# A fourth PSUM pair kept in the ring through the second key projection, and another split of the wk copies between ScalarE and VectorE

## The chip, the cores and the metric

The kernel runs on one core of one Trainium2 chip. The metric is the device time of one execution in microseconds. The kernel before took 290.92 us (median of 3 runs, 290.85 to 291.63).

## The reference, cut to what matters

The program mixes a linear-attention block with a SwiGLU block, for 2048 tokens of width 640.

```python
    def _A_ref(x, wqkv, w_phi, wo):
        ...
        pk = jnp.einsum("bhsd,hdf->bhsf", k, w_phi)
        ...
        phi_k = jnp.concatenate([_softmax(pk, axis=-1), _softmax(-pk, axis=-1)], axis=-1)
        kv = jnp.einsum("bhsf,bhsd->bhfd", phi_k, v)
        ...
    def _B_ref(x, w_gate, w_up, w_down):
        g = _silu(x @ w_gate)
        u = x @ w_up
        return (g * u) @ w_down
    ...
    return g * a + (1 - g) * b
```

Both `k` and `w_phi` are linear, so the kernel multiplies the two weights once, in five chunks of 128 rows ("wk products", steps M0 to M4), and then projects the tokens with the product (steps K0 to K15).

## The kernel before: the parts that matter

The order in which work is issued is a list of steps. F is an FFN item (gate and up products, 512 tokens), M a wk product, V a value product, K a key projection, E a kv sum, Q a query projection, O the attention output, D the down projection, H warm-up matmuls. "I" takes one PSUM pair out of the ring. The loads are issued in their own order (f0, f1, f2 are column ranges of the FFN weights).

```python
LOADS = """
x0 w0 x1 w1 x2 w2 x3 w3 w4 f0 h k0 k1 t4 k2 k3 k4 t5 ... t15 q0 q1 q2 q3
q4 f1 f2
"""
ORDER = """
...
X3 U2.2 U0.3 U1.3 U2.3 U0.4 U1.4 U2.4 V3 Y F0.1 M1 i3 M0 I F0.0 M2 V4 M3 M4 K0 K1 S0 V6 V5 S1 P0
...
"""
```

The eight banks of PSUM are four pairs. A step takes the pair that was used longest ago; the kv sums own pair 3 from E0, the first of them, to the last; step I takes it out of the ring ahead of that.

```python
    ring = {"n": 4, "lru": [0, 1, 2, 3]}
    ...
    def next_pair():
        return used([r for r in ring["lru"] if r < ring["n"] and r not in held][0])
    ...
    def kv_begin():          # step I
        ring["n"] = 3
```

A wk product is six small matmuls and one copy out of PSUM. K0 reads the five products in turn, c = 0 to 4, two matmuls for each, and waits for each copy by itself.

```python
    def premult(which, m):
        pr = next_pair()
        ...
        mm(pairs)
        copy("dve" if which and m % 2 == 0 else "act", wqk[:, which, m, :].rearrange("p (b c) -> p b c", b=2), halves(pr))

    def tok_proj(t, which, split=False):
        pr = next_pair()
        pairs = [(bank(2 * pr + hb, 0, 320), xT[:, t, c, :], wqk[:, which, c, 320 * hb:320 * hb + 320],
                  c == 0, c == 4, False) for c in range(5) for hb in range(2)]
        if split:                                   # K0 only
            for c in range(5):
                mm(pairs[2 * c:2 * c + 2])
        ...
```

The softmax here doesn't subtract the row's maximum and nothing guards it: scores larger than these inputs give would overflow.

## Time and profile before

| | before |
|---|---|
| device time | 290.92 us |
| span of the profiled execution | 288.81 us |
| first matmul of F0.1 | 12.09 us |
| wk products M3, M4 start | 18.73, 19.43 us |
| K0, first kv sum start | 19.75, 27.95 us |
| waits of TensorE after 8 us, by the waits view | one, 0.2 us |

The device time contains about 1.8 us that the span does not; so the span is the part to explain.

From the page of before: span, engine row (busy us, share of the span, instructions), and the chain of work that ended last, by engine.

```profile
span 288.8 us, 4885 instructions
...
PE 285.2 (99%) x1977; PEld 174.7 (60%) x1977; DVE 162.8 (56%) x241; ACT 147.5 (51%) x251; POOL 160.5 (56%) x125
...
PE 96%; DMA 2%; DVE 1%; SPq 0%; ACT 0%; issue 0%
```

In the views PE is TensorE, PEld its weight loads, PEq its sequencer, DVE is VectorE, ACT ScalarE, POOL GpSimd, and SP SyncE, which issues the loads. TensorE sets the time. Its 99% must be read with care. The Trainium skill (Perfetto Trace Analysis, "Tensor Engine Instruction (MATMUL, LD_WEIGHTS)") says that the end of a matmul in the profile is an estimate. So I measure from start to start. The skill (TensorE: Matmul & The Clock Gate, "Wait — 56ns, not 53.3ns?") gives columns / 2.4 GHz + about 2.5 ns for a running array; this trace agrees: 20 matmuls of 320 columns take 2.72 us (0.136 each), 5 of 512 columns take 1.08 us (0.216 each). What a start is later than that is a hole.

The waits view of before, TensorE only:

```profile
engine line waited for: us in total, times, longest us
PE ps L471 <- PEq L773: 0.8, 1, 0.8
PE ps L294 <- DMA wvg<-in_A_wqkv_dram: 0.4, 2, 0.2
PE ps L294 <- DVE wqk L318: 0.2, 1, 0.2
PE ps L294 <- DVE xT L318: 0.2, 1, 0.2
```

The third line is the place that the change aims at. Around it, in the timeline of before (start us, duration us, engine, line, operation, out<-in, count, idle time before it and what ended that):

```profile
17.04 0.48 PE L294 MATMUL ps<-wbd,wT 128*128 128x140 bf16 x6
...
17.35 1.54 PE L294 MATMUL ps<-wvg,xT 128*128 128x320 bf16 x10
17.73 0.59 ACT L312 ACTIVATE us<-ps 128x512 bf16<-128x512 f32 x1
17.86 0.69 DVE L326 SCALAR_TENSOR_TENSOR hT<-hT,ps 128x512 bf16<-128x512 bf16 x1 [1.36 <-ACT hT L312]
18.47 0.81 DVE L318 CAST wqk<-ps 128x640 bf16<-128x640 f32 x1
...
18.73 0.48 PE L294 MATMUL ps<-wbd,wT 128*128 128x140 bf16 x6
18.93 0.71 ACT L312 ACTIVATE v1r<-ps 128x640 bf16<-128x640 f32 x1 [0.60 <-PE ps L294]
19.40 0.32 PEld L294 LDWEIGHTS ps<-wbd,wT 128*128 128x128 bf16 x6 [0.38 <-issue]
19.43 0.47 PE L294 MATMUL ps<-wbd,wT 128*128 128x140 bf16 x6 [0.23 <-DVE wqk L318]
19.53 0.17 ACT L312 ACTIVATE svec<-ps 128x1 f32<-128x1 f32 x1
19.58 0.71 ACT L312 ACTIVATE wqk<-ps 128x640 bf16<-128x640 f32 x1
...
19.75 1.40 PE L294 MATMUL ps<-wqk,xT 128*128 128x320 bf16 x9
19.94 0.82 DVE L318 CAST wqk<-ps 128x640 bf16<-128x640 f32 x1 [0.66 <-PE ps L294]
```

The first line is M2, then V4, M3 (18.73) and M4 (19.43). M1 and M0, one after the other, start about 0.31 us apart, so M4 could have started at 19.04. It starts 0.15 us after VectorE's copy of M2 (18.47 to 19.28): with three pairs M4 must write where M2 was. The profile's own "0.23" is smaller than the hole, because it counts from M3's modelled end; from start to start the hole is 0.39 us.

### The profile page before, as it was taken

What the parts mean: (1) busy time and instruction counts of PE and PEld (TensorE: products, weight loads), DVE (VectorE), ACT (ScalarE), POOL (GpSimd) and SP (SyncE); (2) the same over time, 40 slices, a digit from 0 to 9 for tenths busy, and PEclk for the clock granted to TensorE, in tenths of its full rate; (3) what the DMA queues carried; (4) which work ended last, traced back from release to release, by engine and by line L of the source; (5) the groups of instructions that cost most, each with busy time, mean ns of one, the idle gap of its engine ahead of it and who ended that gap; (6) DMA issues with size and microseconds to landing.
All of it is one profiled execution on the core that took longest, in us unless ns stands there. A gap on an engine that the chain in (4) does not pass through costs nothing.

```text
span 288.8 us, 4885 instructions
## 1 busy us (share of the span) xinstructions
PE 285.2 (99%) x1977; PEld 174.7 (60%) x1977; DVE 162.8 (56%) x241; ACT 147.5 (51%) x251; POOL 160.5 (56%) x125
## 2 busy tenths in 40 slices
PE   8999999999999999999999999999999999999997
PEld 6667777675644445557775546675454446656776
DVE  1256757486468987769992385980316799200000
ACT  1368768676674556574354663224675452234112
POOL 8276899879544798844733348450663649601000
DMA  6966789000010497302373102061020004410101
GB/s 214 174 119 129 108 229 353 5 2 1 0 49 0 75 330 137 70 10 41 62 141 85 20 0 51 2 134 57 2 50 0 2 1 82 92 45 0 48 23 48
DMA packets 48942, 21.61 MB, mean 75 GB/s; under 512 B 39384, under 2 KB 48792, under 8 KB 48920
## 3 DMA queue, kind: packets, MB, share of 16 engines
q1 hardware_dynamic: 48190, 20.62, 31.3%
q10 hardware_dynamic: 730, 0.68, 0.7%
q8 instruction: 16, 0.26, 0.4%
q14 instruction: 6, 0.05, 0.1%
HBM read 9.29 MB, written 2.62 MB: 41 GB/s over the span
## 4 chain that ended last, share of the span: by engine, by line
PE 96%; DMA 2%; DVE 1%; SPq 0%; ACT 0%; issue 0%
PE ps L294 96%; DMA wvg<-in_A_wqkv_dram 2%; SPq L348 0%; DVE wqk L318 0%; DVE hT L326 0%; ACT hT L312 0%; PE ps L306 0%; DVE osb L718 0%
## 5 line engine op out<-in xcount | busy, mean ns | idle before, releaser
L322 POOL TENSOR_TENSOR hT<-hT,us 128x512 bf16<-128x512 bf16 (+1 forms) x56 | 65.6, 1182 | 66.8 <-DVE hT L326 66.6
L326 DVE SCALAR_TENSOR_TENSOR hT<-hT,ps 128x512 bf16<-128x512 bf16 (+1 forms) x56 | 37.5, 683 | 73.5 <-ACT hT L312 61.2
L294 PE MATMUL ps<-xT,wg 128*128 128x512 bf16 x260 | 64.6, 379 | 0.0
L294 PE MATMUL ps<-xT,wu 128*128 128x512 bf16 x260 | 64.6, 379 | 0.0
L294 PE MATMUL ps<-wd,hT 128*128 128x320 bf16 (+2 forms) x462 | 63.9, 295 | 0.0
L312 ACT ACTIVATE hT<-ps 128x512 bf16<-128x512 f32 (+2 forms) x60 | 35.8, 596 | 46.5 <-PE ps L294 46.4
L322 POOL TENSOR_TENSOR ph<-eq,qc 128x1320 bf16<-128x1320 bf16 x16 | 42.4, 2648 | 26.1 <-DVE qc L631 24.0
L294 PEld LDWEIGHTS ps<-wd,hT 128*128 128x128 bf16 x462 | 44.5, 98 | 17.5 <-issue 0.2
L294 PE MATMUL ps<-wqk,xT 128*128 128x320 bf16 x320 | 47.7, 299 | 0.1
L294 PEld LDWEIGHTS ps<-xT,wu 128*128 128x128 bf16 x260 | 25.4, 98 | 30.7
L294 PEld LDWEIGHTS ps<-xT,wg 128*128 128x128 bf16 x260 | 25.0, 98 | 27.8 <-ACT oT L312 0.8
L312 ACT ACTIVATE osb<-ps,omg 128x640 bf16<-128x640 f32 (+2 forms) x17 | 12.9, 758 | 53.7 <-PE ps L294 53.7
L322 POOL TENSOR_TENSOR ekr<-ekr,krec 128x1280 bf16<-128x1280 bf16 x16 | 37.4, 2358 | 5.1 <-DVE krec L336 5.1
L294 PEld LDWEIGHTS ps<-wqk,xT 128*128 128x128 bf16 x320 | 30.5, 98 | 13.3 <-ACT us L312 0.5
L312 ACT ACTIVATE us<-ps 128x512 bf16<-128x512 f32 (+1 forms) x56 | 33.2, 593 | 0.3 <-POOL hT L322 0.2
L312 ACT ACTIVATE eq<-ps 128x640 bf16<-128x640 f32 x32 | 22.4, 704 | 17.3 <-POOL ph L322 10.4
L333 DVE TENSOR_REDUCE ksum<-ekr 128x64 f32<-128x1280 bf16 x16 | 23.5, 1470 | 10.4 <-ACT ekr L312 10.4
L312 ACT ACTIVATE ekr<-ps 128x640 bf16<-128x640 f32 x32 | 22.3, 704 | 8.6 <-PE ps L294 8.1
L294 PE MATMUL ps<-wvg,xT 128*128 128x320 bf16 (+1 forms) x160 | 24.6, 301 | 0.6 <-DMA wvg<-in_A_wqkv_dram 0.4
L333 DVE TENSOR_REDUCE qz<-eq 128x64 f32<-128x1280 bf16 x16 | 23.7, 1478 | 2.2 <-ACT eq L312 2.2
L294 PE MATMUL ps<-wog,oT 128*128 128x320 bf16 (+2 forms) x165 | 24.7, 294 | 0.0
L333 DVE TENSOR_REDUCE qw<-ez 128x64 f32<-128x1280 bf16 x16 | 23.6, 1477 | 0.0
(73 smaller groups left out, 188.6 us busy)
## 6 DMA issues: line engine op xcount, KB each, us to landing
out_dram<-osb SPq DMA_DIRECT2D x15, 160.0 KB, 1.9
wd<-in_B_w_down_dram SPq DMA_DIRECT2D x1, 2080.0 KB, 10.4
wg<-in_B_w_gate_dram SPq DMA_DIRECT2D x1, 1040.0 KB, 9.5
wu<-in_B_w_up_dram SPq DMA_DIRECT2D x1, 1040.0 KB, 10.5
wg<-in_B_w_gate_dram SPq DMA_DIRECT2D x1, 800.0 KB, 5.6
wu<-in_B_w_up_dram SPq DMA_DIRECT2D x1, 800.0 KB, 7.2
wog<-in_A_wo_dram SPq DMA_DIRECT2D x2, 375.0 KB, 7.1
wvg<-in_A_wqkv_dram SPq DMA_DIRECT2D x4, 160.0 KB, 4.5
```

Source lines behind the costliest of these rows:

```text
L294: last = pe.matmul(o, lhsT=l, rhs=r, start=st, stop=sp_, skip_group_check=sk)
L312: return run("act", lambda: act.activation(o, i, func, scale=scale), rd, [o])
L322: return run(e, lambda: eo.tensor_tensor(o, a, b, op), [a, b], [o])
L326: return run("dve", lambda: dve.scalar_tensor_tensor(out=o, in0=a, scalar=s, in1=b, op0=op0, op1=op1), rd, [o])
L333: return run("dve", lambda: dve.tensor_reduce(o, i, AX.X, ALU.add), [i], [o])
```

## The change

Its intent: let the fourth pair work until K1 has taken its own, so that M4 does not wait for M2's copy; and give the copies of M2 and M4 to ScalarE, M3's to VectorE, so that the copies come in the order in which they are wanted. No instruction is added; on balance one copy moves from VectorE to ScalarE.

```diff
-X3 U2.2 U0.3 U1.3 U2.3 U0.4 U1.4 U2.4 V3 Y F0.1 M1 i3 M0 I F0.0 M2 V4 M3 M4 K0 K1 S0 V6 V5 S1 P0
+X3 U2.2 U0.3 U1.3 U2.3 U0.4 U1.4 U2.4 V3 Y F0.1 M1 i3 M0 F0.0 M2 V4 M3 M4 K0 K1 I S0 V6 V5 S1 P0
...
-        copy("dve" if which and m % 2 == 0 else "act", wqk[:, which, m, :].rearrange("p (b c) -> p b c", b=2), halves(pr))
+        copy("dve" if which and m in (0, 3) else "act", wqk[:, which, m, :].rearrange("p (b c) -> p b c", b=2), halves(pr))
```

## The prediction

> **What bounds the kernel.** TensorE. The page's busy table gives PE 285.2 of 288.8 us (99%); the chain of waits is 96% matmuls. The Trainium skill (Perfetto Trace Analysis, Identifying the Most-Contended Engine) warns that matmul busy time says little about headroom, because matmuls are pipelined. So I took the distances between matmul starts in the timeline: 512-column matmuls follow each other at about 0.215 us, 320-column ones at about 0.135 us, nearly everywhere. After the first loads (about 8 us) I find one real hole, 0.39 us before the last wk product M4 (start 19.43 us, "DVE wqk"), one of 0.24 us at 128.9 us, and some below 0.1 us.
>
> **What makes the hole.** With the ring cut to three pairs before F0.0, M4 must write into M2's pair. Timeline: M2 runs at 17.04 us; its copy belongs to VectorE, which is first busy with F0.0's gate product (17.86 to 18.55) and copies M2 from 18.47 to 19.28. M3 is issued by about 19.04; M4 starts at 19.43, some 0.15 us after the copy's end.
>
> **What the change does.** The matmuls and their order stay the same; one wk copy moves from VectorE (0.82 us) to ScalarE (0.71 us).
> 1. Fourth pair until K1. Following the least-recently-used ring by hand, M4 then takes F0.0's pair, whose last reader ends at 18.55, and K0 takes M2's. M4 can start straight after M3, at about 19.04 (its weights landed at about 18.5), and K0 at about 19.35 instead of 19.75.
> 2. New split (VectorE: M0, M3; ScalarE: M1, M2, M4). K0 reads the wk products as its chunks 0 to 4. ScalarE copies M2 at about 18.2 to 18.9, in idle time before V4's copy, then M4 at about 19.58 to 20.29. VectorE is free for M3 at about 19.25 to 20.07. Chunk 3 is due at 19.35 + 6 x 0.135 = 20.16, chunk 4 at about 20.43; adding 0.15 us from a copy's end to the matmul, they are there at about 20.2 and 20.44. So K0 may stall 0 to 0.1 us. The split mainly frees M2's pair (now K0's) by about 19.0 instead of 19.28, which would be just before K0 needs it.
>
> **On the critical path:** estimate 0.39 - 0.04 = about 0.35 us. After K1 the assignment of pairs is the old one with names exchanged, so no wait is new. Later loads land at least 0.5 us before use: V6's token block at 21.3 us against 22.1, the last FFN weights at 51.4 against about 53. So PE's later work should move forward by 0.35 us, to the end.
>
> **Predicted time:** 290.92 - 0.35 = 290.57 us, say 290.6; range 290.1 to 291.0 (runs of before differ by 0.8 us among themselves, so the gain is of the size of the noise). Faster by over 2%: 0.5%; within 2%: 98.5%; slower by over 2%: 1%.
>
> **Right, if:** M4 follows M3 without the hole, and "PE <- DVE wqk" goes from PE's waits, or shrinks below 0.1 us inside K0; K0 starts at about 19.35 us; later PE landmarks (first kv sum, 27.95 us; Q7, 128.9 us) come 0.3 to 0.4 us earlier; span about 288.45 us. Wrong, if the hole reappears inside K0 (waiting for the copies of M3 or M4), or the lead is lost at a later load or at 128.9 us.
>
> **What would make it wrong:** loads arriving later in the first 20 us, which shift everything by some tenths; copies slower than 0.71 and 0.82 us when ScalarE and VectorE read PSUM together, making K0 wait; drift between sessions larger than the gain.

## The result, and the profile after

| | before | changed |
|---|---|---|
| device time, 6 runs each, median | 290.86 us | 290.91 us |
| lowest, highest | 290.07, 291.63 | 290.13, 291.47 |
| span of the profiled execution | 288.81 us | 288.36 us |
| F0.1's first matmul to the end of the span | 276.72 us | 276.32 us |

The ratio is 1.0004, with a 95% interval of 0.9981 to 1.0027. The timing shows no difference; a gain of 0.40 us would be a ratio of 0.9986, which lies inside the interval. The trace, on the other hand, shows the forecast gain.

The waits view of the changed kernel, TensorE only:

```profile
engine line waited for: us in total, times, longest us
PE ps L471 <- PEq L773: 0.8, 1, 0.8
```

The timeline of the changed kernel, same columns:

```profile
16.99 0.48 PE L294 MATMUL ps<-wbd,wT 128*128 128x140 bf16 x6
...
17.82 0.69 DVE L326 SCALAR_TENSOR_TENSOR hT<-hT,ps 128x512 bf16<-128x512 bf16 x1 [1.37 <-ACT hT L312]
18.16 0.71 ACT L312 ACTIVATE wqk<-ps 128x640 bf16<-128x640 f32 x1
...
18.68 0.79 PE L294 MATMUL ps<-wbd,wT 128*128 128x140 bf16 x12
18.88 0.71 ACT L312 ACTIVATE v1r<-ps 128x640 bf16<-128x640 f32 x1
19.20 0.82 DVE L318 CAST wqk<-ps 128x640 bf16<-128x640 f32 x1 [0.69 <-PE ps L294]
...
19.31 1.79 PE L294 MATMUL ps<-wqk,xT 128*128 128x320 bf16 x12
19.48 0.17 ACT L312 ACTIVATE svec<-ps 128x1 f32<-128x1 f32 x1
19.53 0.71 ACT L312 ACTIVATE wqk<-ps 128x640 bf16<-128x640 f32 x1
```

M3 and M4 are now one unbroken group of twelve matmuls (18.68), K0 starts at 19.31, and its matmuls follow each other without a break. M2's copy is ScalarE's (18.16), M3's is VectorE's (19.20), M4's is ScalarE's (19.53). The two traces differ by 0.05 us when F0.1 starts (12.09 and 12.04) and by 0.45 us at the first kv sum (27.95 and 27.50), at Q7 (128.91 and 128.46) and at the end.

So the question is the reverse of the usual one: the mechanism is plain in the trace, and the time does not show it. Where is it lost? Three theories stood at this point.

- **A:** the 0.40 us are saved in every execution, and the spread between executions (1.6 us) hides them. The spread comes from the first 12 us.
- **B:** the hole or its removal depends on the execution; in ordinary ones nothing is saved.
- **C:** TensorE is earlier, but waits for something later in some executions.

### The profile page after: what moved, and what is told of

It is laid out like the page before. It is cut to its first block, busy times and chain, and to the rows that moved or that the text cites. A ratio compares the mean times of both kernels' runs of the same rounds, so it can differ in the third digit from the quotient of the medians.

```text
span 288.4 us, 4884 instructions
## 1 busy us (share of the span) xinstructions
PE 285.5 (99%) x1977; PEld 175.2 (61%) x1977; DVE 162.1 (56%) x240; ACT 148.1 (51%) x252; POOL 160.5 (56%) x125
## 4 chain that ended last, share of the span: by engine, by line
PE 99%; DVE 0%; issue 0%
PE ps L294 97%; PE ps L471 1%; PE ps L306 1%; DVE osb L718 0%
```

## The experiments

In each I measured two things: the timed runs, and in the trace the distance from F0.1's first matmul to the end of the span, which leaves out the start.

### 1. More warm-up matmuls: does the spread come from the first loads?

88 warm-up matmuls ahead of the first transposes, the same edit in both kernels, so that the loads are there before TensorE asks.

```diff
-    def warm():
+    def warm(count=NWARM):
...
-            for _ in range(NWARM):
+            for _ in range(count):
...
-        "H": lambda i: warm(), ...
+        "H": lambda i: warm(90 if i == 12 else NWARM), ...
```

For the kernel before:

> The kernel before, with 88 more warm-up matmuls ahead of the first transposes, so that the first loads have landed before TensorE needs them. Theory A (the hole of 0.39 us is there in every execution and its removal reaches the end; the spread of up to 1.6 us between executions comes from the arrival of the first loads): 5 to 9 us slower than before, spread of its runs far below that of before (under 0.4 us), TensorE waits between 4 and 9 us of the old time scale gone, the 0.39 us hole before M4 still there. Rival B (spread is not from the loads, but from later, or from the launch): spread stays about 1 us. Rival C (the hole itself depends on when the loads come): the hole changes or is gone.

For the changed kernel:

> The changed kernel with the same 88 warm-up matmuls. Theory A: against q_before in the same rounds 0.3 to 0.5 us shorter, now outside the spread of both; no hole before M4 or K0. Rival B or C (the gain of the profile is lost again in ordinary executions): q_after and q_before agree within 0.1 us.

Measured: before with the edit 295.97 us median (295.23 to 296.33, 4 runs), changed with the edit 295.8 us (294.75 to 296.26, 5 runs). From F0.1 to the end: 276.72 and 276.32 us, to 0.01 us what they were. The hole before M4 is there in one (0.39 us) and gone in the other.

So the hole belongs to the kernel and not to the moment at which loads arrive: B lost ground. But the spread did not shrink (1.1 and 1.5 us), so my source for it was wrong, and the timed difference (0.28 us between the means) lies within it. The traces show what I had missed. In both, the warm-up matmuls start 0.107 us apart at first and 0.059 us apart later; the last slow one is at 5.49 us in one and at 6.77 us in the other, and the first value product follows at 10.54 and 11.11 us. The moment at which TensorE doubles its rate differs from execution to execution. The Trainium skill (TensorE: Matmul & The Clock Gate, "What's actually happening") says this too: the array runs at half rate until one busy window of about 3.4 us has passed, and the window runs freely, so that the moment depends on where in it the first matmul falls. Here it comes 4.6 and 5.9 us after the first matmul (0.84 us).

The timelines of TensorE in two executions with the ordinary start show it. Before (full rate from about 5 us on):

```profile
0.84 2.29 PE L471 MATMUL ps<-const-bfloat16-1.0 128*128 128x128 bf16 x20 [0.84 <-PEq L773]
...
5.60 0.44 PE L294 MATMUL ps<-wvg,xT 128*128 128x320 bf16 x2
6.24 0.72 PE L294 MATMUL ps<-wvg,xT 128*128 128x320 bf16 x4 [0.20 <-DVE xT L318]
6.80 0.44 PE L306 MATMUL ps<-ident,xs 128*128 128x128 bf16 x5
```

The ring alone (experiment 2), where the half rate lasted until 8.5 us:

```profile
0.84 2.29 PE L471 MATMUL ps<-const-bfloat16-1.0 128*128 128x128 bf16 x20 [0.84 <-PEq L773]
...
5.59 0.74 PE L306 MATMUL ps<-ident,xs 128*128 128x128 bf16 x5
...
6.34 1.83 PE L294 MATMUL ps<-wvg,xT 128*128 128x320 bf16 x6
7.97 0.74 PE L306 MATMUL ps<-ident,xs 128*128 128x128 bf16 x5
...
13.43 0.81 PE L294 MATMUL ps<-xT,wg 128*128 128x512 bf16 x3
```

A group of five transposes takes 0.74 us in the second, even at 7.97 us, and 0.44 us in the first from 6.80 us on; and F0.1 (last line) starts at 13.43 in place of 12.09.

### 2. The fourth pair alone

```diff
-... i3 M0 I F0.0 M2 V4 M3 M4 K0 K1 S0 ...
+... i3 M0 F0.0 M2 V4 M3 M4 K0 K1 I S0 ...
```

> Fourth pair until K1, with the old split of the copies (VectorE M0, M2, M4; ScalarE M1, M3). Measured in the trace from the first matmul of F0.1 to the end, before has 276.72 us and the changed kernel 276.32. Mine: M4 follows M3 at once, but K0 must take M2's pair, whose VectorE copy ends as late as before, so a hole of about 0.1 us comes before K0, and one of 0.1 to 0.2 us inside it (M3's copy on ScalarE waits for V4's); so 276.5 to 276.65, a third to a half of the gain. Rival (the prediction on record: the old split would have been about as early): within 0.1 us of the changed kernel. The timed ratio cannot tell these apart: within 0.3% of before.

Measured: F0.1 to the end 276.50 us, between before (276.72) and the changed kernel (276.32); 290.7 us median (290.12 to 291.69, 4 runs), ratio 0.9998 (0.9974 to 1.0021). From its timeline:

```profile
19.82 0.82 DVE L318 CAST wqk<-ps 128x640 bf16<-128x640 f32 x1
...
20.33 0.54 PE L294 MATMUL ps<-wbd,wT 128*128 128x140 bf16 x7
...
20.70 1.57 PE L294 MATMUL ps<-wqk,xT 128*128 128x320 bf16 x9
20.87 0.17 ACT L312 ACTIVATE svec<-ps 128x1 f32<-128x1 f32 x1
20.90 0.82 DVE L318 CAST wqk<-ps 128x640 bf16<-128x640 f32 x1 [0.27 <-PE ps L294]
20.92 0.71 ACT L312 ACTIVATE wqk<-ps 128x640 bf16<-128x640 f32 x1
...
21.68 0.39 PEld L294 LDWEIGHTS ps<-wqk,xT 128*128 128x128 bf16 x4 [0.34 <-ACT wqk L312]
```

M4 follows M3 at once. K0 starts at 20.70, straight after M4: the 0.1 us hole before it that I expected is not there, although M2's VectorE copy (19.82 to 20.64) frees its pair only 0.06 us earlier. What is there is a hole of 0.17 us inside K0, at 21.68: chunk 3 waits for ScalarE's copy of M3 (20.92 to 21.63), which had to queue behind V4's two copies. So the pair alone gives 0.22 us of the 0.40.

### 3. The new split alone

```diff
-        copy("dve" if which and m % 2 == 0 else "act", ...
+        copy("dve" if which and m in (0, 3) else "act", ...
```

> The new split alone, with the ring cut to three pairs before F0.0. M2's copy on ScalarE ends at about 18.9 us, so M4 needn't wait for its pair. Mine: the hole moves to K0, which takes V4's pair, read by ScalarE until about 19.7; K0 starts at 19.7 to 19.75 as before; from F0.1 to the end 276.65 to 276.75 us: no gain. Rival (the split is what took the hole away, the fourth pair is not needed): 276.3 to 276.4. The timed ratio: within 0.3% of before.

Measured: 290.51 us median (290.32 to 290.72, 4 runs), ratio 0.9985 (0.9968 to 1.0002). F0.1 to the end: 277.18 us, 0.46 longer than either theory had it. From its timeline:

```profile
18.40 0.81 PE L294 MATMUL ps<-wbd,wT 128*128 128x140 bf16 x12
18.60 0.71 ACT L312 ACTIVATE v1r<-ps 128x640 bf16<-128x640 f32 x1
...
19.20 0.17 ACT L312 ACTIVATE svec<-ps 128x1 f32<-128x1 f32 x1
...
19.41 0.25 PEld L294 LDWEIGHTS ps<-wqk,xT 128*128 128x128 bf16 x3 [0.39 <-ACT svec L312]
19.42 0.45 PE L294 MATMUL ps<-wqk,xT 128*128 128x320 bf16 x2 [0.21 <-ACT svec L312]
```

The hole has moved. M3 and M4 are one group, since ScalarE empties M2's pair early; but with three pairs K0 must take V4's, which ScalarE reads until 19.37, and a hole of 0.37 us stands before K0. K0 and the first kv sum come 7.66 and 15.86 us after F0.1, exactly as in before: by this split alone nothing is won. Pair and split need each other.

The other 0.46 us are a second hole, at F0.8. The lines of the DMA queue and of TensorE from the timelines of this run:

```profile
39.79 1.38 SPq L348 DMA_DIRECT2D wu<-in_B_w_up_dram  x1
...
52.28 1.24 PE L294 MATMUL ps<-xT,wg 128*128 128x512 bf16 x5 [0.29 <-issue]
```

The load of the last up-weights, issued at 39.79 us, took 12.4 us to land (the longest of the three loads of `wu`), so until 52.19. F0.8, whose step waits for both of its weights before its first matmul, starts at 52.28; from start to start the hole is 0.46 us. The profile names no releaser for it, so that it is this load is read from the two times. That is a wait as theory C has it.

| trace, ordinary start | load of F0.8 landed | F0.8 started |
|---|---|---|
| before | 51.44 | 52.15 |
| changed | 51.15 | 51.70 |
| changed, second trace (experiment 6) | 51.53 | 51.74 |
| fourth pair alone | 52.97 | 53.28 |
| new split alone | 52.19 | 52.28, after a wait of 0.46 |

The slack is 0.2 to 0.7 us where there is any; a lead of 0.40 us is of its size. But the rows do not show that the earlier TensorE comes, the likelier it waits: the changed kernel came at 51.70 and 51.74 us without a wait, the new split alone was due at 51.82 (52.28 less the hole) and waited. The landing moves by itself, from 51.15 to 52.97 us.

### 4. A paced start: is the rate change the source of the spread?

VectorE first does six reduces of 1.48 us on scratch data, ahead of its copies, and there are 73 more warm-up matmuls after the first transposes. The same edit in both kernels.

```diff
+    def pace():
+        memset("dve", ez[:, 0, :], 1.0)
+        for _ in range(6):
+            reduce(qw[:, 0, :], ez[:, 0, :].rearrange("p (g d) -> p g d", d=DH))
...
-H0 H1 H2 ...
+a H0 H1 H2 ...
...
+        "H": lambda i: warm(75 if i == 11 else NWARM), "a": pace,
```

For the kernel before:

> The kernel before with a paced start: six VectorE reduces of 1.48 us (on a scratch tile) ahead of VectorE's first copies, and 73 more warm-up matmuls after the first transposes, so that the first value product starts at about 11 us, set by VectorE, when TensorE has its full rate and the loads are there. Six traces so far: from F0.1's first matmul on, all is fixed to 0.01 us (but for one load wait), while F0.1 itself starts at 11.76 to 13.43 us; TensorE's matmuls run at half rate until 3.9 to 9.0 us, at a moment that differs between executions. Theory D (the spread of the runs is the moment at which TensorE's rate doubles, and first loads): with the start paced the spread of the runs falls from 1.0-1.6 us to under 0.4 us; time about 5 to 7 us above before; hole of 0.39 us before M4 still there. Rival (the spread is launch or end of the program): the spread stays at 1 us or more.

For the changed kernel:

> The changed kernel with the same paced start. Theory A+D: shorter than r_before in the same rounds by 0.40 us (0.3 to 0.5), and now the two sets of runs hardly overlap. Rival (the gain of the profile does not hold in ordinary executions): equal within 0.1 us.

(The 9.0 us in the first of these texts is a short wait that I took for half rate; the last half-rate matmul there starts at 8.50 us.)

Measured: 303.5 us median (303.09 to 303.86, 4 runs) and 303.16 us (302.99 to 303.69, 4 runs). F0.1 to the end: 276.73 and 276.32 us. The start was later than I wanted: the warm-up matmuls themselves waited for VectorE's first copy until 11.54 us, so the first value product came at 17.7 us. After the 7.5 us without matmuls they ran at half rate again, and the last slow one is at 15.46 us in one trace and at 15.78 in the other, so the edit did not fix the moment of the rate change. The spread was 1.57 us in 11 runs of before of the same rounds, and 0.77 and 0.70 us here, not under the 0.4 I had expected. But 4 runs span less than 11 by their number alone: the standard deviation fell only from 0.46 to 0.37 and 0.33 us. So the timing does not show that the start makes the spread; the traces show that F0.1 moves. The means differ by 0.24 us; the two sets of runs overlap.

### 5. The late load brought forward

f2 holds the columns that F0.8 needs; f1 is not needed before F1.2, at 83 us in the trace of before (the text below says about 90).

```diff
-q4 f1 f2
+q4 f2 f1
```

For the kernel before:

> The kernel before, with the last two FFN weight loads swapped (columns 896 to 1727, which F0.8 needs first, ahead of columns 256 to 895, not needed before about 90 us). In five traces with the ordinary start the load that F0.8 needs landed at 51.2 to 53.0 us, with F0.8 due at 51.7 to 53.5; one execution waited 0.46 us. Theory E (in executions with an early start the load of F0.8 takes back what TensorE has won): landing about 46 us, no wait at F0.8 in the trace; time equal to before or up to 0.3 us shorter, fewer long runs. Rival (that wait is rare): equal within 0.1 us. The swap might slow nothing.

For the changed kernel:

> The changed kernel with the same swap of the two loads. The changed kernel reaches F0.8 0.4 us earlier, so it is more exposed to that load. Theory E: no wait at F0.8, F0.1 to the end 276.32 us, time 0.4 us under f_before, 0.3 to 0.7 us under before. Rival (the exposure is rare): 0.4 us under before, like the changed kernel itself would be without noise; the runs' spread is as large as before either way, so the interval may still include no change.

Measured: before with the swap 291.11 us median (290.06 to 292.54, 6 runs), ratio 1.0019 (0.9995 to 1.0043); changed with the swap 290.18 us (290.12 to 290.55, 5 runs), ratio 0.9988 (0.9974 to 1.0003). The load that F0.8 needs landed at 48.4 and 47.9 us (about 46 was expected), 3.6 and 4.1 us before F0.8 started; F0.1 to the end 276.72 and 276.34 us. The changed kernel with the swap is, by its mean, 0.39 us under before of the same rounds, the size that the trace gives, and its runs lie close together; but its interval still includes 1. The swap gave before nothing: its runs are widely spread and in the mean 0.46 us longer than before's, which the theory does not explain.

### 6. The changed kernel again

No edit; more runs, on another chip.

> The changed kernel itself, once more, to add runs on another chip. Measured so far: from F0.1's first matmul to the end 276.32 us against 276.72 in before, the time before F0.1 11.76 to 13.43 us in both. Theory A (0.40 us in every execution, hidden in the spread of the start): F0.1 to end 276.32 unless the last FFN load is late; mean of the runs 0 to 0.8 us under before, all runs of the case taken together nearer to 0.4. Rival (no gain in ordinary executions): all runs taken together show 0.0.

(The 11.76 and 13.43 us in this text are the starts of the two half-variants; in the traces of the two kernels, with and without the swap, F0.1 had started at 11.90 to 12.30 us.)

Measured: 290.61 us median, but 290.15 to 294.2 over 6 runs; ratio 1.0016 (0.9978 to 1.0054). F0.1 to the end 276.33 us. All 12 runs of the changed kernel have a median of 290.84 us, the 38 runs of before in the four sets of rounds one of 290.80 us. I had written that with all runs together A shows nearer to 0.4 us, and the rival 0.0. By the median it shows 0.0; by the mean the changed kernel is 0.25 us longer, with a standard error of 0.34 us (without its one run of 294.2 us, 0.03 us shorter).

### 7. The load made later on purpose (failed as a test)

One load of wq chunk 0 repeated ahead of the FFN loads, in both kernels.

```diff
-q4 f1 f2
+q4 q0 f1 f2
```

For the kernel before:

> The kernel before with one weight load (of wq chunk 0, the same data) repeated ahead of the FFN weight loads, so that the load which F0.8 needs comes about 1.3 us later (landing at about 52.5 to 54.3 us, against F0.8 due at about 51.8 to 53.5). Theory E (that load can take the gain back): a wait of 0 to 2 us at F0.8; F0.1 to the end above 276.72 by just that wait; time 0 to 1.5 us above before.

For the changed kernel:

> The changed kernel with the same repeated load. Theory E: it comes to F0.8 0.4 us earlier and waits 0.4 us longer for the same landing, so the time from F0.8 to the end is what counts in both: time equal to l_before within 0.2 us, where both wait. Rival (the gain stays, whatever the load does): 0.4 us under l_before.

Measured: 295.8 us (293.18 to 296.12, 6 runs) and 296.97 us (295.81 to 297.45, 4 runs), ratios 1.0155 ("same") and 1.0206 ("unclear"). F0.1 to the end: 282.54 and 282.36 us. My edit was wrong: all loads precede all steps in program order, so R0, the step that reads this weight, waited for the repeated load; the wait was there (line from the waits view of before with this edit) and not at F0.8:

```profile
PE ps L294 <- DMA wTq<-in_A_wqkv_dram: 4.1, 1, 4.1
```

In the changed kernel that wait was 3.7 us. After it TensorE ran at half rate for 3.3 to 3.4 us in both (in the changed kernel only from some 0.9 us after it went on). The two runs therefore say little of F0.8. They show once more that the start differs: the first value product came at 5.04 and 5.18 us, but the last half-rate matmul before F0.1 at 3.69 and 8.57 us, and F0.1 at 12.07 and 13.50 us. The means of the timed runs differ by 1.4 us in the same sense, against both expectations. And the wait cost more than itself: from start to start the holes were 4.3 and 3.9 us, while F0.1 to the end grew by 5.8 and 6.0 us. The windows view of before with this edit (busy us and instructions of PE, PEld, DVE, ACT, POOL, granted TensorE clock, DMA share, GB/s):

```profile
36.00:41.00 5.00, 1.34 (x19) 0.96 (x16) 1.79 (x2) 1.19 (x4) 4.47 (x3) 1.00 0.88 127
41.00:44.00 3.00, 2.55 (x23) 1.98 (x24) 0.00 (x0) 0.70 (x1) 3.00 (x2) 0.56 0.92 293
44.00:47.00 3.00, 3.00 (x29) 2.12 (x28) 0.30 (x1) 1.46 (x3) 0.01 (x1) 0.87 1.07 380
```

The clock of 0.56 in the second line is the half rate after the hole.

### 8. Both, and the hole before Q7

The changed kernel with the swap of experiment 5, and with F0.11 and Q6 exchanged, against the hole of 0.24 us before Q7.

```diff
-... B4 Q6 F0.11 C4 O0.0 ...
+... B4 F0.11 Q6 C4 O0.0 ...
-q4 f1 f2
+q4 f2 f1
```

> The changed kernel, with the FFN loads swapped as in f_after, and with the order of F0.11 and Q6 exchanged, so that Q7 takes a pair whose readers have ended 1.4 us sooner. The hole of 0.24 us before Q7 (at 128.5 us) is in every trace. If the reader of F0.11's pair makes that hole, it goes and F0.1 to the end falls from 276.32 to about 276.1 us; if it is a cost of changing from the 64-row products to Q7, it stays. Time 0.3 to 0.9 us under before (0.6 by the trace), the start's spread permitting.

Measured: 290.7 us median (290.29 to 290.85, 5 runs), ratio 0.9995 (0.9983 to 1.0007); F0.1 to the end 276.68 us in place of 276.34. The hole before Q7 stayed (0.27 us), and a new one of 0.39 us opened before the down projection, at 131.4 us. I had counted the ring wrongly: Q7 takes the pair of whichever step came last before the three O steps, now Q6, whose two ScalarE exponentials end only at 128.24 us, just before Q7 starts at 128.30. In the changed kernel Q7 starts 0.14 us after VectorE's last reading of F0.11's pair (128.32 us), so that pair remains the likely cause of the first hole. The hole at 131.4 us ends 0.10 us after ScalarE's last copy of oT (130.29 to 131.31), which the down projection reads; in the changed kernel too the projection starts 0.11 us after this copy (130.13 to 131.15). From F0.1 on, the copy comes 0.35 us later with the exchange, because ScalarE has Q6's exponentials first. This is read from the timelines; no run tests it. The trace's loss against the changed kernel of experiment 5 is 0.34 us; the means of the timed runs, of different rounds, differ by 0.38 us.

## Why the prediction was right or wrong

Where the span comes from, in all eight traced executions without an edit to the start or a load made late (us; half rate is read from the distance to the next start, waits left out):

| kernel | last matmul at half rate | F0.1 starts | F0.1 to the end | span |
|---|---|---|---|---|
| before | 4.98 | 12.09 | 276.72 | 288.81 |
| before, loads swapped | 3.79 | 11.90 | 276.72 | 288.62 |
| changed | 5.74 | 12.04 | 276.32 | 288.36 |
| changed, again | 5.48 | 12.08 | 276.33 | 288.41 |
| changed, loads swapped | 5.53 | 12.30 | 276.34 | 288.64 |
| fourth pair alone | 8.50 | 13.43 | 276.50 | 289.94 |
| new split alone | 3.93 | 11.76 | 277.18 | 288.94 |
| both and Q7 | 5.10 | 11.85 | 276.68 | 288.53 |

- **The hole and its cause: right, shown.** The hole of 0.39 us before M4 is in all five traces that have before's ring and split, and in none of the changed kernel. It is M2's copy and the missing pair: it goes when either is changed (experiments 2 and 3).
- **The size, 0.35 us: right, 0.40 us measured** in the trace from F0.1 to the end, in four traces of before's ring and split against five of the changed one, all without another wait (276.72 to 276.73 against 276.32 to 276.34; they are those of before and changed, and of experiments 1, 4, 5 and 6). The term of 0.04 us for a stall inside K0 was too large; K0 runs without a break. The time from a copy's end to the matmul, which I took as 0.15 us, was as short as 0.06 us in experiment 2.
- **What the split does: wrong in its reason.** The prediction said that it "mainly frees M2's pair". Experiment 2 shows that K0 did not wait for that pair without the split; it waited 0.17 us for the copy of M3. The split is worth 0.18 us of the 0.40 by taking that copy away from ScalarE's queue behind V4's.
- **"Later loads land at least 0.5 us before use ... to the end": wrong as a general statement.** I took the slack from one trace, and there against F0.8's up product ("about 53"), while the step already waits for that load before its gate product at 52.15: the slack was 0.71 us, not 1.6. In others it was 0.2 and 0.3 us, and in one it was negative, with 0.46 us lost. So in an execution with a late load a part of the gain can be given back at F0.8. In how many executions this happens is open: no kernel has more than two traced executions, and none of the changed kernel's traces shows it.
- **The time, 290.6 us: 290.91 us measured, inside the range of 290.1 to 291.0.** That says little: before's own 290.92 lies inside the range as well, so no gain at all would have landed there. The forecast gain was not seen in the time, and the prediction had said that it is of the size of the noise. A source of the noise that it did not foresee is TensorE's start at half rate: where the last half-rate matmul came at 8.50 and 8.57 us (the fourth pair alone; the changed kernel of experiment 7), F0.1 started at 13.43 and 13.50 us; in the other eight traces, where it came by 5.74 us, at 11.76 to 12.30. Among those eight there is no clear order, so something else moves F0.1 too, probably the first loads.

What of A, B and C remains? B is refuted for the traced executions: in the nine traces of the two kernels without another wait, F0.1 to the end is fixed to 0.02 us. A and C remain together. The three pairs of kernels in which F0.8 has slack by construction (experiments 1, 4 and 5) have the changed one shorter by 0.28, 0.24 and 0.85 us in the mean; weighted by their scatter this is 0.38 us with a standard error of 0.18. The pair with the load in its old place shows nothing in 12 runs. That fits C, but I drew this grouping up after seeing the numbers, and the runs are few. Whether the load at F0.8 or plain scatter hides the gain in the ordinary timing is not settled. The changed kernel with the two loads swapped (290.18 us, ratio 0.9988, interval 0.9974 to 1.0003) is kept as the candidate for its trace, 0.40 us less from F0.1 to the end and its slack of 4.1 us at F0.8. The timing cannot rank the variants: the new split alone has a lower ratio (0.9985, interval 0.9968 to 1.0002) with a trace in which nothing is gained.

## What to carry to other kernels

When a change is worth less than the spread of the runs, time it in the trace between two fixed landmarks behind the noisy part: here 0.40 us showed to 0.02 us in single traces, while a dozen timed runs did not resolve it. A ring of buffers and the engine that empties it are one mechanism: the extra buffer alone gave half, the better split alone gave nothing, because the wait moved to the next step. And before counting on a lead to reach the end, look up the slack of every later load in more than one trace.

## What the Trainium skill lacked or had wrong

- TensorE: Matmul & The Clock Gate, "What you observe", puts the rise to full rate around 4 us into sustained matmul activity, give or take 0.5 us. In experiment 1 the matmuls follow each other without a break from 0.84 us on, and the last half-rate one starts 4.6 and 5.9 us later; in experiment 4, after the hole, 3.9 and 4.2 us later. With waits for the first loads in between it started at 3.8 to 8.5 us in eight executions, and the start of the FFN moved by 1.7 us with it and with the loads. The page's statement that the moment varies from run to run is confirmed; the range that it gives is too narrow here.
- The same page, "What's actually happening", calls the ramp under 1% of a typical span and not worth fitting. Here the earliest and the latest start of F0.1 lie 1.7 us apart, 0.6% of the time, so the statement stands; but this is larger than the change under study, and no page says that it sets a floor for what timing can resolve.
- The same page warns that the clock-gate events of a trace are unreliable; no page says that the granted clock in the profile can miss the initial half rate altogether: the window from 0.90 to 2.90 us of before shows a clock of 1.00, while its matmuls of 128 columns start 0.107 us apart, twice the later 0.056. After the wait of 4 us in experiment 7 it did show it (0.56).
- Perfetto Trace Analysis, "Optimization Strategy", advises to look for the gaps on the bounding engine and what ends them. The page says elsewhere that matmul ends are estimates, but not what follows for the gaps: the profile put 0.23 us before M4, from start to start it is 0.39 us.
